# Pooled and local attention with a SoLU feed-forward layer on one core: the local probabilities of batches 3 to 7 transposed by DMA and VectorE instead of TensorE, with a new order of all engines

## The chip, the cores and the metric

The kernel runs on one core of one Trainium2 chip. The metric is the device time in microseconds (us) of one execution. The kernel before was timed three times: 622.41 us in the median, 622.0 lowest and 624.12 highest.

## The reference

Eight batches of eight heads, 576 positions, 64 values a head. Attention is computed twice and added: once between positions that were averaged in groups of four (144 of them, softmax over all, then each result repeated four times), and once locally, where a position sees only its neighbours at a distance below four.

```python
out_d = sm_attn(q_d, k_d, v_d)                      # 144 pooled positions
out_up = np.repeat(out_d, factor, axis=2)           # factor = 4
mask = np.abs(pos[:, None] - pos[None, :]) < factor
scores = np.where(mask, scale * q @ k.T, -1e9)
attn = softmax(scores)                              # local
attn_out = out_up + attn @ v
# x: 4608 tokens x 512
h = x @ w_in                                        # 512 -> 1024
solu = h * softmax(h)
ln = (solu - mean) / sqrt(var + 1e-6) * g_ln
out = ln @ w_out                                    # 1024 -> 512
```

The inputs are fp32, the feed-forward weights arrive as 64-bit words.

## The kernel before

**Local attention.** The 576 positions of a batch are covered by ten windows of 64, two windows to a unit, so five units a batch (class `Local`; a name such as `sc_3_1` is the local score tile of batch 3, unit 1). `by_tensor` (L690) makes a unit in these steps: 16 small matmuls for the scores into PSUM (`sc`, L698); on VectorE the mask is added (`pl`, L710) and the maximum taken (L715); GpSimd subtracts it (L717); ScalarE takes the exponential (L719); VectorE sums and inverts (L722, L726); GpSimd multiplies (L728). Then TensorE transposes the probabilities in four 128x128 pieces into PSUM (`plt`, L738), ScalarE copies them to SBUF (`plT`, L741), and 16 small matmuls multiply them with v (`xp`, L748). The result is written to x by ScalarE (`accumulate`, L587) or added by VectorE (L589). The rows of v for this form, `vw`, are loaded in four DMAs a unit with the two windows swapped for half of the heads (`load_vw`, L316).

A second form, `by_blocks` (L606), stands in the file but isn't used: `ON_TENSOR = 8` (L595) sends all eight batches through `by_tensor`.

**Pooled attention** (class `Pooled`): four units a batch, score tile `sd`, transposed tile `pdt`, result `po`. In batches 0 and 1 the pooled v comes from matmuls (`pv`, L490), later from GpSimd (`vs`, `vd`, L517 and L520). q and k are transposed on TensorE in batches 0 to 2 (`qp`, `kp`, L570), by VectorE's 32x32 transposes in batches 3 to 7 (L460, L464).

**Feed-forward.** 36 tiles of 128 tokens. Each is split into two parts of reduced width (`xh`, `xl`), multiplied in 24 matmuls of 512 columns (`h`, L848), normalised by all three vector engines, written to DRAM (`u`, L891) and read back in four DMAs as blocks (`v`, L924), which VectorE transposes (L945); after a split (`uh`, L951; `ul`, L953) 24 matmuls make the output (`o`, L967), which ScalarE scales (L974) and SyncE stores (L976). `v` has two buffers, `vw` five, `plT` two, the probabilities `pl` four.

**Order.** The work is a list of about two thousand steps, and the table `ORDER` gives the order in which they are written out; each engine executes its own in that order and waits for what is not ready. All DMAs are issued by SyncE, one queue in that same order: a DMA that waits holds up all DMAs behind it. The table `FILL` names PSUM tiles with a number n: ahead of the first matmul into such a tile, TensorE does n matmuls of the identity with itself (`idle_...`, L237) whose result nobody reads.

Of the kernel before, what the change touches and what calls it, by code (L numbers as in the profile page):

```python
# [139 lines left out]
def pooled_local_attention_then_solu_ffn(  # L140
# [451 lines left out]

    ON_TENSOR = 8  # L595

    class Local:

# [513 lines left out]
```

## Time and profile before

| | |
|---|---|
| time, median of 3 | 622.41 us (622.0 to 624.12) |
| time of the profiled execution | 623.45 us |
| its span, first to last instruction | 621.7 us |
| TensorE busy (matmul) | 599.2 us, 96% |
| VectorE, ScalarE, GpSimd busy | 391.9, 373.3, 374.5 us, 63%, 60%, 60% |
| moved by DMA | 91.97 MB, 148 GB/s in the mean |
| granted TensorE clock, mean | 0.989 |

The profile is of one execution. Busy time of TensorE is that of its matmul records; they overlap, so the time that a piece of work takes on TensorE is read from its start to the start of the next piece. An fp32 matmul can stand in the trace as two records: 16 local score matmuls give 32, and one `idle` matmul gives two. Matmuls of the reduced type (`h`, `o`) and transposes give one. SPq is SyncE issuing a DMA.

### The profile page before, as it was taken

To read this page: it belongs to the slowest core of one execution; us is meant where nothing else is said; L and a number is where in the kernel's file an instruction comes from. 1 tells how busy PE (TensorE), PEld (TensorE's weight loads), DVE (VectorE), ACT (ScalarE), POOL (GpSimd) and SP (SyncE) were. 2 spreads that over 40 slices of the span, in tenths; PEclk is the share of its full clock that TensorE was granted. 3 is DMA by queue.
4 is the path that set the end of the run, shared out by engine and by line. 5 is a ranking of instruction groups with operands and counts; after the bars stand their busy time and mean duration, and the time that the engine had idled before them with its cause. 6 is when DMAs were issued, how large, how long until landed. Compare 5 with 4: busy or idle time off the path is not lost.

```text
span 621.7 us, 15270 instructions
## 1 busy us (share of the span) xinstructions
PE 599.2 (96%) x5932; PEld 472.2 (76%) x5932; DVE 391.9 (63%) x687; ACT 373.3 (60%) x810; POOL 374.5 (60%) x566
## 2 busy tenths in 40 slices
PE   6969899999999999999999999999999999999997
PEld 5847768777777777777777877777777777788876
DVE  4877599997446784578537783778367444443540
ACT  4656668966556557556755585656655675454451
POOL 7553476769835895479636973689546964242210
PEclk9998799999999999999999999999999999999999
DMA  9969678987976279735883897433542232224220
GB/s 192 203 150 210 145 215 186 170 205 191 189 190 161 91 180 193 186 112 147 194 190 105 196 183 181 161 104 89 168 126 86 71 101 86 85 90 159 92 101 35
DMA packets 205608, 91.97 MB, mean 148 GB/s; under 512 B 169568, under 2 KB 194400, under 8 KB 205536
## 3 DMA queue, kind: packets, MB, share of 16 engines
q1 hardware_dynamic: 205536, 91.00, 60.5%
q8 instruction: 47, 0.77, 0.5%
q14 instruction: 25, 0.20, 0.1%
HBM read 63.18 MB, written 27.79 MB: 146 GB/s over the span
## 4 chain that ended last, share of the span: by engine, by line
PE 76%; POOL 7%; SPq 4%; DMA 4%; ACT 3%; DVE 3%; issue 2%; POOLq 0%; ACTq 0%
PE o L967 28%; PE h L848 28%; PE xp L748 3%; PE po L830 3%; PE sc L698 3%; PE plt L738 3%; SPq L316 3%; PE sd L774 2%; PE pdt L809 2%; POOL vs L517 1%; POOL pl L728 1%; POOL pl L717 1%; PE kp L570 1%; DMA v<-u 1%; PE pv L490 1%
## 5 line engine op out<-in xcount | busy, mean ns | idle before, releaser
L967 PE MATMUL o<-wo_h,uh 128*128 128x512 f32 x288 | 117.2, 407 | 0.3
L848 PE MATMUL h<-wi_h,xh 128*128 128x512 f32 x288 | 117.3, 407 | 0.0
L967 PE MATMUL o<-wo_l,uh 128*128 128x512 f32 x288 | 114.3, 397 | 0.0
L848 PE MATMUL h<-wi_l,xh 128*128 128x512 f32 x288 | 114.2, 396 | 0.0
L848 PE MATMUL h<-wi_h,xl 128*128 128x512 f32 x288 | 114.1, 396 | 0.0
L953 POOL TENSOR_TENSOR ul<-v,uh 128x512 fp32r<-128x512 f32 x58 | 74.5, 1291 | 27.2 <-ACT uh L951 25.3
L856 DVE TENSOR_REDUCE nmx<-h 128x1 f32<-128x1024 f32 x36 | 43.7, 1214 | 59.3 <-PE h L848 59.3
L967 PE MATMUL o<-wo_h,ul 128*128 128x512 f32 x288 | 79.0, 396 | 0.0
L967 PEld LDWEIGHTS o<-wo_h,uh 128*128 128x128 f32 x288 | 54.3, 189 | 13.7 <-issue 0.5
L848 PEld LDWEIGHTS h<-wi_h,xh 128*128 128x128 f32 x288 | 54.3, 188 | 13.5 <-issue 0.8
L967 PEld LDWEIGHTS o<-wo_h,ul 128*128 128x128 f32 x288 | 54.3, 189 | 13.3
L848 PEld LDWEIGHTS h<-wi_h,xl 128*128 128x128 f32 x288 | 54.3, 188 | 13.2
L848 PEld LDWEIGHTS h<-wi_l,xh 128*128 128x128 f32 x288 | 54.3, 189 | 11.6
L967 PEld LDWEIGHTS o<-wo_l,uh 128*128 128x128 f32 x288 | 54.3, 188 | 11.6
L1001 POOL TENSOR_TENSOR xl<-x,xh 128x512 fp32r<-128x512 f32 (+1 forms) x40 | 47.0, 1179 | 24.5 <-ACT xh L998 24.2
L728 POOL TENSOR_TENSOR pl<-pl,rsl 128x512 f32<-128x512 f32 x40 | 43.2, 1086 | 19.5 <-DVE rsl L726 13.4
L945 DVE STREAM_TRANSPOSE v<-v 128x512 f32<-128x512 f32 x70 | 46.3, 691 | 11.1 <-DMA v<-u 11.0
L860 ACT ACTIVATE e<-h,nmx 128x1024 f32<-128x1024 f32 x36 | 40.1, 1113 | 21.8 <-DVE nmx L856 21.4
L885 ACT ACTIVATE e<-e,nmu 128x1024 f32<-128x1024 f32 x35 | 40.2, 1148 | 20.5 <-POOL nmu L868 20.4
L951 ACT ACTIVATE uh<-v 128x512 fp32r<-128x512 f32 x70 | 43.5, 624 | 14.6 <-DVE v L945 11.6
L717 POOL TENSOR_TENSOR pl<-pl,mxl 128x512 f32<-128x512 f32 x40 | 42.9, 1079 | 15.1 <-DVE mxl L715 14.8
L998 ACT ACTIVATE xh<-x 128x512 fp32r<-128x512 f32 (+1 forms) x40 | 22.8, 584 | 46.8 <-PE h L848 39.5
(117 smaller groups left out, 1152.5 us busy)
## 6 DMA issues: line engine op xcount, KB each, us to landing
u<-e SPq DMA_DIRECT2D x35, 512.0 KB
v<-u SPq DMA_DIRECT2D x140, 128.0 KB
vw<-in_v_dram SPq DMA_DIRECT2D x160, 64.0 KB
out_dram<-osb SPq DMA_DIRECT2D x36, 256.0 KB
vs<-in_v_dram SPq DMA_DIRECT2D x24, 288.0 KB
qm<-in_q_dram SPq DMA_DIRECT2D x20, 288.0 KB
km<-in_k_dram SPq DMA_DIRECT2D x20, 288.0 KB
w<-in_moe_w_out_dram SPq DMA_DIRECT2D x8, 512.0 KB
```

Of the source, the lines that this page charges most:

```text
L717: nc.gpsimd.tensor_tensor(out=pl, in0=pl, in1=max_bc, op=ALU.subtract)
L728: nc.gpsimd.tensor_tensor(out=pl, in0=pl, in1=rs.unsqueeze(3).broadcast_to([P, NPR, 2, W]), op=ALU.mult)
L848: nc.tensor.matmul(hps[:, n, :], src[:, cc, :], wt[:, cc, n * 512:(n + 1) * 512], start=(cc == 0 and src is xh and wt is wi_h), stop=(cc = ...
L856: nc.vector.tensor_reduce(out=nmx, in_=hf, op=ALU.max, axis=AX.X, negate=True)
L860: nc.scalar.activation(e, hf, AF.Exp, bias=nmx, scale=1.0, accum_out=se)
L885: nc.scalar.activation(e, e, AF.Identity, bias=nmu, scale=1.0)
L945: nc.vector.transpose(vg, vg)
L951: nc.scalar.activation(uh, tp, AF.Copy)
L953: (nc.vector if v is None or i in LATE else nc.gpsimd).tensor_tensor(out=ul, in0=tp, in1=uh.bitcast(F32), op=ALU.subtract)
L967: nc.tensor.matmul(o, src[:, j, :], wt[:, 4 * g + j, :], start=(g == 0 and j == 0 and src is uh and wt is wo_h), stop=(g == 1 and j == 3 a ...
L998: nc.scalar.activation(h, src, AF.Copy)
L1001: nc.gpsimd.tensor_tensor(out=l, in0=src, in1=h.bitcast(F32), op=ALU.subtract)
```

## The change

Batches 3 to 7 use `by_blocks`; batches 0 to 2 stay as they were. In `by_blocks` the scores are written to PSUM in another arrangement, so that each 32 keys of all heads lie together (L610 to L631); the steps up to the product on GpSimd are the same in number and size, with one small VectorE instruction more (1e-9 added to the sums, L649 before). The transposition differs: eight DMAs of 32 partitions by 256 elements move the 32x32 blocks to their places in SBUF (L660 before, L661 after), and one VectorE transpose of 128x512 turns each block in itself (L666, L667). TensorE's four `plt` transposes and ScalarE's copy go. The `xp` matmuls then take 64 columns instead of 56 or 58. v's rows are loaded as they lie, in two DMAs a unit instead of four, the same bytes (L308, L309). All lines behind the tables are one higher in the program after.

```diff
 FILL = {
-    "kp_0_2": (3, "o"), "qp_0_3": (2, "o"), "kp_0_3": (2, "o"), "pv_0_1": (3, "o"),
-    "po_0_0": (8, "o"), "sd_0_2": (2, "o"), "po_0_3": (3, "o"), "plt_0_0": (12, "o"),
-    "xp_0_0": (5, "o"), "sc_0_1": (6, "o"), "sc_0_3": (13, "o"), "xp_0_3": (2, "o"),
-    "o_2": (6, "o"), "pv_1_0": (2, "o"), "sc_1_0": (3, "o"), "sc_1_2": (2, "o"),
-    "plt_1_2": (8, "o"), "xp_1_2": (4, "o"), "sc_1_3": (3, "o"), "po_1_3": (3, "h"),
-    "plt_2_2": (10, "o"), "o_34": (3, "h"), "o_35": (5, "h"),
+    "qp_0_1": (11, "o"), "kp_0_1": (5, "o"), "qp_0_2": (3, "o"), "kp_0_3": (3, "o"),
+    "pv_0_0": (2, "o"), "pv_0_1": (10, "o"), "pdt_0_0": (2, "o"), "sd_0_1": (3, "o"),
+    "pdt_0_1": (3, "o"), "sd_0_2": (3, "o"), "plt_0_0": (4, "o"), "xp_0_0": (6, "o"),
+    "xp_0_2": (7, "o"), "xp_0_4": (2, "o"), "h_1": (2, "o"), "h_3": (4, "o"),
+    "pv_1_0": (7, "o"), "sc_1_2": (5, "o"), "xp_1_3": (2, "o"), "pdt_1_0": (9, "o"),
+    "sd_1_2": (9, "o"), "sd_1_3": (3, "o"), "po_1_3": (4, "h"), "o_4": (8, "o"),
+    "o_8": (15, "o"), "qp_2_2": (3, "o"), "pdt_2_1": (3, "o"), "o_14": (13, "o"),
+    "pdt_4_1": (3, "o"), "o_34": (3, "h"), "o_35": (5, "h"),
 }
...
-0 33 7 14 1 2 3 21 4 5 8 6 135 40 9 143 10 41 42 15 151 11 12 16 13 17 28 43 18 19 44 22 20 50
+28 33 29 0 135 30 1 143 2 3 31 136 4 5 6 34 137 7 138 139 144 140 40 145 141 146 14 41 142 42
...
-    ON_TENSOR = 8
+    ON_TENSOR = 3
```

The new table changes all engines' order. The numbers at the end of a name below only count the program's tiles.

TensorE in batch 3, between feed-forward tile 8's first half and tile 6's second, before:

```order
L848 MATMUL h_8_3015<-wi_h_113,xh_8_2647 128x512
L848 MATMUL h_8_3015<-wi_l_114,xh_8_2647 128x512
L848 MATMUL h_8_3015<-wi_h_113,xl_8_2648 128x512
L748 MATMUL xp_3_0_3072<-plT_3_0_3028,vw_3_0_2209 64x58 x16
L698 MATMUL sc_3_4_3095<-kT_3_2171,qT_3_2170 64x64 x16
L738 MATMUL plt_3_1_3119<-ident_82,pl_0_103 128x128 x4
L967 MATMUL o_6_3128<-wo_h_115,uh_6_0_2947 128x512
```

The same place after:

```order
L849 MATMUL h_8_3049<-wi_h_113,xh_8_2652 128x512
L849 MATMUL h_8_3049<-wi_l_114,xh_8_2652 128x512
L849 MATMUL h_8_3049<-wi_h_113,xl_8_2653 128x512
L672 MATMUL xp_3_0_3104<-plT_3_0_2831,vw_3_0_2235 64x64 x16
L616 MATMUL sc_3_4_3127<-kT_3_2232,qT_3_2231 64x2x32 x16
L968 MATMUL o_6_3155<-wo_h_115,uh_6_0_3012 128x512
L968 MATMUL o_6_3155<-wo_l_116,uh_6_0_3012 128x512
```

The row of the four transposes is gone; `xp` has 64 columns and the scores go out in two stripes of 32.

SyncE's queue around the read-back of tile 8 (`v_8`), ahead of the q and k loads of batch 5, before:

```order
L891 DMA u_8_3187<-e_8_3141 128x1024
L316 DMA vw_4_1_3219<-in_v_dram 64x4x64 x4
L924 DMA v_8_3265<-u_8_3187 32x4x256 x4
L976 DMA out_0_dram<-osb_6_3209 128x512
L296 DMA qm_5_3295<-in_q_dram 32x72x32 x4
L296 DMA km_5_3296<-in_k_dram 32x72x32 x4
```

And after:

```order
L892 DMA u_8_3240<-e_8_3170 128x1024
L309 DMA vw_4_1_3254<-in_v_dram 64x8x64 x2
L977 DMA out_0_dram<-osb_6_3249 128x512
L661 DMA plT_3_3_3278<-pl_2_105 32x256 x8
L325 DMA vs_4_1_4_3370<-in_v_dram 72x4x256
L661 DMA plT_3_4_3377<-pl_3_106 32x256 x8
L892 DMA u_9_3422<-e_9_3374 128x1024
L309 DMA vw_4_2_3447<-in_v_dram 64x8x64 x2
L977 DMA out_0_dram<-osb_7_3445 128x512
L925 DMA v_8_3482<-u_8_3240 32x4x256 x4
L925 DMA v_9_3505<-u_9_3422 32x4x256 x4
L297 DMA qm_5_3514<-in_q_dram 32x72x32 x4
```

`v_8` went from two places behind `u_8` to nine: two groups of eight block DMAs, the write of tile 9 and the store of tile 7 stand in between. `o_8` has 15 fill matmuls ahead of it in the new table, and none before.

SyncE's first DMAs, before:

```order
L552 DMA qm_0_124<-in_q_dram 96x6x64 x2
L552 DMA km_0_125<-in_k_dram 96x6x64 x2
L552 DMA qm_0_124<-in_q_dram 96x6x64 x2
L552 DMA km_0_125<-in_k_dram 96x6x64 x2
L552 DMA qm_0_124<-in_q_dram 96x6x64 x2
```

And after:

```order
L317 DMA vw_0_0_124<-in_v_dram 64x4x64 x4
L317 DMA vw_0_1_161<-in_v_dram 64x4x64 x4
L553 DMA qm_0_166<-in_q_dram 96x6x64 x2
L553 DMA km_0_167<-in_k_dram 96x6x64 x2
L363 DMA stage_172<-in_moe_w_in_dram 64x1024 x2
```

Eight DMAs of v's rows moved ahead of the first q and k. Further down, the loads of batch 1's first three `vw` stand behind one piece of w_out (`w64_10`) and one `vs` more than before.

193 rows, old and new, of the table ORDER are left out of this document.

## The prediction

> **What bounds the kernel now.** I read the page first, then the busy time of the engines in four stages, then TensorE's and SyncE's timelines at single places. The page names TensorE:
>
> ```profile
> span 621.7 us, 15270 instructions
> PE 599.2 (96%) x5932; PEld 472.2 (76%) x5932; DVE 391.9 (63%) x687; ACT 373.3 (60%) x810; POOL 374.5 (60%) x566
> ```
>
> I cut the span where the first and the fifth feed-forward tile (h_0, h_4) begin on TensorE, 80.90 and 144.19 us:
>
> ```profile
> 80.90 0.50 PE L848 MATMUL h<-wi_h,xh 128*128 128x512 f32 x1
> ...
> 144.19 0.48 PE L848 MATMUL h<-wi_h,xh 128*128 128x512 f32 x1
> ```
>
> By the order of both programs TensorE does the same 972 matmuls, fill left out, ahead of h_4. So the change can be counted stage by stage. Busy time by stage, with the granted clock, the DMA share and GB/s at the end of a row:
>
> ```profile
> 0.00:80.90 80.90, 66.58 (x950) 54.09 (x950) 55.12 (x102) 45.90 (x121) 44.00 (x69) 0.92 0.94 182
> 80.90:144.20 63.30, 62.08 (x737) 48.84 (x735) 57.14 (x96) 49.96 (x92) 44.24 (x56) 1.00 0.83 192
> 144.20:510.00 365.80, 362.82 (x3685) 284.12 (x3683) 234.43 (x419) 226.18 (x510) 255.89 (x371) 1.00 0.60 150
> 510.00:621.70 111.70, 107.69 (x567) 85.19 (x566) 45.16 (x72) 51.24 (x90) 30.37 (x73) 1.00 0.27 90
> ```
>
> Up to 80.9 us TensorE idles 14.3 us and runs at 0.92 of its clock: this stage waits for loads (DMA share 0.94). From 144.2 us on it idles 3.0 of 365.8 us: there the time is what TensorE has to do, and all batches that the change touches lie there.
>
> **The change part by part.** *The transposes that go.* A slot between two feed-forward tiles looks like this:
>
> ```profile
> 214.55 0.69 PE L748 MATMUL xp<-plT,vw 64*64 64x58 f32 x32
> 215.06 0.65 PE L698 MATMUL sc<-kT,qT 64*64 64x64 f32 x32
> 215.65 0.66 PE L738 MATMUL plt<-ident,pl 128*128 128x128 f32 x4
> 216.06 0.47 PE L967 MATMUL o<-wo_h,uh 128*128 128x512 f32 x1
> ```
>
> From start to start plt takes 216.06 - 215.65 = 0.41 us, a unit. Five batches of five units: 25 x 0.41 = 10.25 us less on the engine that bounds this stage.
>
> *Wider xp.* 58 columns take 0.51 us here, the 64-column scores 0.59. By columns, 0.51 x 64/58 gives 0.05 more; the ends are 0 and 0.08. I take 0.04: 25 x 0.04 = 1.0 us (0 to 2.0). The scores keep their number and width.
>
> *Fill in this stage.* Before, 16 fill matmuls stand behind h_4, ahead of plt_2_2 and o_2:
>
> ```profile
> 151.08 2.50 PE L237 MATMUL idle_plt<-ident 128*128 128x128 f32 x20
> 154.55 0.66 PE L738 MATMUL plt<-ident,pl 128*128 128x128 f32 x4 [0.97 <-POOL pl L728]
> 155.04 1.50 PE L237 MATMUL idle_o<-ident 128*128 128x128 f32 x12
> 156.70 0.47 PE L967 MATMUL o<-wo_h,uh 128*128 128x512 f32 x1
> ```
>
> They go, and with them (154.55 - 151.08) + (156.70 - 155.04) = 5.1 us; it is 0 if the waits below them stay, which GpSimd's 0.97 us hints at. I take the 5.1, as the order has other work there. The new table puts 42 into this stage (o_4 8, pdt_2_1 3, o_8 15, pdt_4_1 3, o_14 13). Ten took 2.50 us, so 0.25 each: 42 x 0.25 = 10.5 us. Fill costs its time whether TensorE would have waited there or not; it is lost either way, and a longer wait adds to it. So this one term eats the whole of the 10.25.
>
> Is there a wait under it? For o_8 I think so. In the new order v_8 is issued behind the store of tile 7; from the end of o_7 the chain is ScalarE's output 0.68, four issues, the landing, two VectorE transposes 2 x 0.69, the first split 0.62. The rows, from the groups of instructions (busy, mean ns, idle before), SyncE's timeline and the chain that ended last:
>
> ```profile
> L967 PEld LDWEIGHTS o<-wo_h,uh 128*128 128x128 f32 x288 | 54.3, 189 | 13.7 <-issue 0.5 <-ACT osb L974 0.5
> L945 DVE STREAM_TRANSPOSE v<-v 128x512 f32<-128x512 f32 x70 | 46.3, 691 | 11.1 <-DMA v<-u 11.0
> L951 ACT ACTIVATE uh<-v 128x512 fp32r<-128x512 f32 x70 | 43.5, 624 | 14.6 <-DVE v L945 11.6
> ...
> 258.65 1.92 SPq L924 DMA_DIRECT2D v<-u  x4
> ...
> 260.15 6.03 DMA v<-u
> ...
> 209.02 5.61 PE h L848 x24
> ```
>
> With 1.92 for the issues and a landing between 2 (a choice, low) and 6.03 us: 0.7 + 1.9 + 2 to 6 + 1.4 + 0.6 = 6.6 to 10.6 us. TensorE has h_10 meanwhile, 5.6 us, and four small groups (xp, sd, xp, pdt) of about 0.5 us as in the slot above, 7.6 us; the fill's 15 x 0.25 bring it to 11.4. So the fill covers the wait and I add none.
>
> *The other engines.* VectorE gets 25 transposes of 0.69 us (row L945, the same tile size) and 25 small sums, 0.2 us by the row of the 128x8 reciprocal:
>
> ```profile
> L726 DVE RECIPROCAL rsl<-sml 128x8 f32<-128x8 f32 x40 | 8.1, 203 | 1.4
> L741 ACT ACTIVATE plT<-plt 128x512 f32<-128x512 f32 x40 | 23.7, 592 | 7.6 <-PE plt L738 7.4
> L728 POOL TENSOR_TENSOR pl<-pl,rsl 128x512 f32<-128x512 f32 x40 | 43.2, 1086 | 19.5 <-DVE rsl L726 13.4
> L1001 POOL TENSOR_TENSOR xl<-x,xh 128x512 fp32r<-128x512 f32 (+1 forms) x40 | 47.0, 1179 | 24.5 <-ACT xh L998 24.2
> ```
>
> That is 22 us on an engine that is busy 234 of 365.8 us; ScalarE loses 25 x 0.59 = 15 us. Both are under TensorE's work: zero. If VectorE waits for a late block transfer, the maximum of the next h tile stands behind it in its order, which is part of the first rival. GpSimd's two steps keep their size; with the other stride they cost between their 1.09 and the 1.18 us of a subtraction of two full operands, 25 x 2 x 0.09 = 5 us on an engine with 110 us to spare.
>
> *SyncE.* Each unit adds eight block DMAs of 32 KB. Nearest are the four pieces of v<-u, 128 KB each: 1.92 / 4 = 0.48 us an issue; and the four of vw, 64 KB each, 2.58 / 4 = 0.65. So it isn't the size that sets it, and I take 0.48: 3.8 us a unit (to 5.2). v's rows in half as many issues save between 0 (if it goes by rows) and 1.3 us:
>
> ```profile
> 416.76 2.58 SPq L316 DMA_DIRECT2D vw<-in_v_dram  x4
> ...
> SPq L891 <- ACT e L885: 133.7, 22, 12.1
> SPq L976 <- ACT osb L974: 37.3, 18, 7.8
> SPq L324 <- POOL vd L520: 25.0, 9, 5.6
> SPq L924 <- DMA u<-e: 19.8, 16, 2.7
> ```
>
> So 25 x (2.5 to 5.2) = 62 to 130 us more in the queue, against 215.8 us that it spends in these four waits. In the sum it fits: zero, with the first rival as the price if it doesn't. The Trainium skill speaks against this: "DMA: Bandwidth & Descriptors", Anatomy of one DMA, gives about 2.0 us of fixed cost to a DMA, and its Rules for kernel authors say that below 64 KB one mostly pays overhead; as an estimate from that page, eight paid one after another are 16 us a unit, 400 us in all, some 184 more than these waits hold, and the time would be near 800 us. The row of four pieces in 1.92 us shows that they are issued without paying that in turn, so the sum goes by the row.
>
> *The early stages.* Eight vw DMAs, 2 x 2.58 = 5.2 us, stand ahead of the first q load, so TensorE starts about 5 us later. 23 fill matmuls more stand ahead of h_0 and 3 more up to h_4 (26 x 0.25 = 6.5 us). Against this: two of the waits before h_0, and a halved clock twice:
>
> ```profile
> 46.58 4.55 PE L490 MATMUL pv<-vw,sums 64*72 64x256 f32 x20 [4.07 <-ACT vd L502]
> ...
> 68.51 0.85 PE L748 MATMUL xp<-plT,vw 64*64 64x58 f32 x42 [2.19 <-issue]
> ...
> 40.00:60.00 20.00, 15.64 (x143) 11.01 (x140) 11.78 (x22) 9.68 (x29) 5.89 (x5) 0.83 1.12 209
> 60.00:80.00 20.00, 17.17 (x382) 14.67 (x382) 12.37 (x25) 12.31 (x31) 10.02 (x9) 0.83 0.75 169
> ```
>
> What fixes h_0, I think, is the pv group of batch 1 just ahead of it on TensorE in both orders: it needs batch 1's first three vw. Ahead of these the new queue has a w_out piece and a vs more:
>
> ```profile
> vw<-in_v_dram SPq DMA_DIRECT2D x160, 64.0 KB
> vs<-in_v_dram SPq DMA_DIRECT2D x24, 288.0 KB
> w<-in_moe_w_out_dram SPq DMA_DIRECT2D x8, 512.0 KB
> ```
>
> 512 + 288 KB are 4.4 us at the stage's 182 GB/s. But vw runs at SyncE's pace, 64 KB in 0.65 us or some 100 GB/s, so part of it hides. Ends: -9 us (waits and clock gone, the late start absorbed) and +10 (late start and fill paid in full). I take a value near the middle, as the same loads end the stage: +0.6, and 3 x 0.25 = 0.75 up to h_4.
>
> *Sum:* -10.25 + 1.0 - 5.1 + 10.5 + 0.6 + 0.75 = -2.5 us. The profiled execution took 623.45 us, 1.75 beside its span, so 620.9 on its scale; it lies 1.04 above the median of the three. On the median: 622.41 - 2.5 = 619.9, said as 620.0 us.
>
> **The rivals.** *Slower: the one DMA queue.* By the new order 11 of the 25 groups of block DMAs stand directly ahead of a v<-u group. Each holds it up for 3.8 us, plus the time it waits itself for GpSimd's product: 42 us if no tile had slack. For slack speaks that the list of TensorE's waits has none for a split v (uh); against it, that VectorE waits for v already, for 11 of 35 tiles:
>
> ```profile
> DVE v L945 <- DMA v<-u: 11.0, 11, 2.7
> ```
>
> If a quarter of the 42 gets through, 10 us: 630 us. It decides where a read-back has less than 3.8 us in hand. Chance 0.25.
>
> *Faster: fill replaces idle time and keeps the clock.* If TensorE's 4.07 us wait goes (v is there early) and the two stretches at 0.83, 2 x 0.17 x 20 = 6.8 us of clock, go too, stage one is 4.07 + 6.8 - 5.2 = 5.7 us shorter instead of 0.6 longer: 613.6 us. For it: 10 fills instead of 3 at that very pv. Against it: the stage ends with loads. The Trainium skill, "TensorE: Matmul & The Clock Gate", HAM oscillation, says that an idle stretch above some 3.4 us halves the clock; the trace agrees at the 4.07 us wait, and by it this rival is what the denser fill would do. Chance 0.2.
>
> *No change at all,* because the transposes lay under other work, I hold for excluded: TensorE idles 3.0 us in 365.8. Nor can the change fail to do what it says; the order shows the rows gone.
>
> **How the numbers follow.** Forecast 0.5: a band of about 6 us around 620.0, of which 0.26 lies below 620.5, 0.15 within 0.3% of 622.41 (620.5 to 624.3, what a measurement of this kernel can just tell apart), 0.09 above. Slower rival 0.25, all above. Faster rival 0.2, all below. The rest of 0.05 goes 0.03 to the same and 0.02 to slower. Faster 0.46, same 0.18, slower 0.36. Low end 609: the faster rival's 613.6, less the 1.0 for xp and 3.6 of the late start. High end 632: the slower rival's 630 and xp's upper end with another microsecond of early fill. Outside remain less than 2 in 10.
>
> **What would show it.** Right: between h_4 and the end the span shrinks by 3 to 5 us; a slot without plt is 0.4 us shorter; the o_8 fill is followed by little idle time; h_0 starts at 79 to 85 us. Wrong: TensorE waits for uh or for plT in the list of waits, several us each, with SyncE's waits on the block DMAs in front (the slower rival); or h_0 starts by 76 us with a clock of 1.0 from 40 to 80 us (the faster one). I am wrong in the sign's ground if fill in the new profile covers nothing, that is, if the operands of o_8 and o_14 were ready long before the fill ended.

## The result and the profile after

The changed kernel takes 632.53 us in the median of four runs (630.18 to 634.61), the kernel before, run beside it, 622.2 us: a ratio of 1.0145, 95% interval 1.0107 to 1.0182. It is slower by about 10 us; the forecast was 620.0, within 609 to 632.

The profiled execution took 630.18 us, the shortest of the four, so its span shows 6.4 us of the 10. The page of the changed kernel (span, busy time, the chain that ended last by engine):

```profile
span 628.1 us, 15648 instructions
PE 599.5 (95%) x5936; PEld 471.1 (75%) x5936; DVE 423.6 (67%) x737; ACT 360.5 (57%) x785; POOL 376.8 (60%) x566
PE 62%; SPq 14%; DVE 8%; DMA 7%; ACT 3%; POOL 3%; issue 3%; DVEq 0%; POOLq 0%; ACTq 0%
```

TensorE is busy as long as before, 599.5 against 599.2 us, though 100 transposes are gone: fill took their place. SyncE issuing DMAs is 14% of the chain that ended last, with the block DMAs as SyncE's largest part, 5%.

The busy time by stage shows where the 6.4 us came from. The cuts are h_0, h_4, h_17 on TensorE. After (a row: stretch, length, busy time of TensorE, its weight loads, VectorE, ScalarE, GpSimd; clock, DMA share, GB/s):

```profile
0.00:83.09 83.09, 67.42 (x997) 55.62 (x997) 59.77 (x104) 46.76 (x121) 44.23 (x68) 0.96 0.91 179
83.09:149.50 66.41, 63.63 (x745) 49.74 (x741) 56.69 (x99) 51.72 (x95) 50.61 (x66) 1.00 0.75 183
149.50:353.44 203.94, 199.89 (x2003) 155.99 (x2002) 142.24 (x253) 111.66 (x254) 130.35 (x188) 1.00 0.70 168
353.44:628.10 274.66, 268.52 (x2206) 209.74 (x2200) 164.95 (x284) 150.33 (x316) 151.65 (x246) 1.00 0.49 136
```

The two later stages of the kernel before, with the new cut at its own h_17:

```profile
144.19:343.56 199.37, 196.92 (x1996) 154.16 (x1994) 130.20 (x232) 120.21 (x270) 135.82 (x198) 1.00 0.69 165
343.56:621.70 278.14, 273.61 (x2259) 215.16 (x2257) 149.40 (x260) 157.21 (x329) 150.45 (x246) 1.00 0.41 116
```

Stage by stage: 83.09 - 80.90 = +2.2 us, 66.41 - 63.29 = +3.1, 203.94 - 199.37 = +4.6, 274.66 - 278.14 = -3.5. So the change gains in the last stage, where 14 of the 25 units stand, and loses in all three ahead of it, in the third although 11 units' transposes went there too. Within the third stage the loss stands at three tiles, those with fill ahead of their `o`: from h_6 to h_7 (o_4) it takes 3.7 us longer than before, from h_10 to h_11 (o_8) 4.7 and from h_16 to h_17 (o_14) 2.4; the tiles between them are shorter by 6.1 us in sum. The second profile of the changed kernel (run e12 below) has the same shape: h_4 7.0 us behind the kernel before, h_17 12.7, the end 9.3.

A slot without the transposes, on TensorE's timeline after:

```profile
220.16 0.69 PE L672 MATMUL xp<-plT,vw 64*64 64x64 f32 x32
220.68 0.65 PE L616 MATMUL sc<-kT,qT 64*64 64x64 f32 x32
221.26 0.51 PE L968 MATMUL o<-wo_h,uh 128*128 128x512 f32 x1
```

The 0.41 us of plt are gone, and the wider xp takes 220.68 - 220.16 = 0.52 us, against 0.51 before. The waits that changed, from the list of waits after:

```profile
PE qp L571 <- POOL sums L265: 10.0, 1, 10.0
DVE v L946 <- DMA v<-u: 20.4, 12, 3.3
ACT uh L952 <- DVE v L946: 22.4, 15, 4.6
```

TensorE starts at 10.0 instead of 4.40 us. VectorE waits 20.4 us for read-backs, 11.0 before, ScalarE 22.4 for VectorE's transposed v, 11.6 before. SyncE's queue at the point that the prediction worked out, the read-back of tile 8 (the last row holds those of tiles 8 and 9, four DMAs each):

```profile
236.54 4.94 SPq L661 DMA_DIRECT2D plT<-pl  x8
242.23 0.33 SPq L892 DMA_DIRECT2D u<-e  x1
242.60 2.50 SPq L309 DMA_DIRECT2D vw<-in_v_dram  x2
245.19 0.57 SPq L977 DMA_DIRECT2D out_dram<-osb  x1
245.80 3.81 SPq L925 DMA_DIRECT2D v<-u  x8
```

Eight block DMAs take 4.94 us, 0.62 each, not 0.48; the trace's 25 groups take 4.94 to 7.69 us, 137 in sum. The two issues of vw take 2.50 us here, nearly the 2.58 of four before, but this place is an exception: over the 25 units two issues take 1.27 to 2.64 us, 41.6 in sum, where the four of before took 2.57 to 3.78, 72.9 in sum. And what TensorE does meanwhile, with the fill at o_8:

```profile
248.98 0.53 PE L810 MATMUL pdt<-ident,pd 64*72 64x64 f32 x12
249.44 3.62 PE L238 MATMUL idle_o<-ident 128*128 128x128 f32 x30
253.21 0.48 PE L968 MATMUL o<-wo_h,uh 128*128 128x512 f32 x1
```

The fill is followed by 0.15 us of idle time: it is about as long as the wait below it. ScalarE's split for o_8 (`uh_8`) ends 0.37 us before o_8 begins; in the kernel before, without fill, it ended 8.2 us before. Which work makes it late is the question of the experiments.

A step that can make it late shows in ScalarE's order at tile 14 (instructions in sequence, the lists of the two programs). Before:

```
L951 ACTIVATE uh_14_0_4710<-v_14_4611 128x512
L951 ACTIVATE uh_14_1_4721<-v_14_4611 128x512
L860 ACTIVATE e_16_4756,se_16_4757<-h_16_4662,nmx_16_4718 128x1024
```

After:

```
L861 ACTIVATE e_16_4827,se_16_4828<-h_16_4723,nmx_16_4784 128x1024
L817 ACTIVATE pdT_4_3_4825<-pdt_4_3_4812 72x6x48
L952 ACTIVATE uh_14_0_4833<-v_14_4756 128x512
L901 ACTIVATE e_15_4588,m2_15_4837<-e_15_4588 128x1024
L952 ACTIVATE uh_14_1_4842<-v_14_4756 128x512
```

The split of tile 14, which TensorE needs for o_14, stood ahead of the exponential of tile 16 and stands behind it now; the same has happened to uh_8 and the exponential of tile 10, and to uh_4 and that of tile 6. Behind h_4 these are the only three tiles of the new order whose split stands behind the exponential of two tiles later, and o_4, o_8 and o_14 are the only `o` behind h_4 to which the new table adds fill. That exponential can't begin until TensorE has finished h_16, and o_14 comes right behind h_16. ScalarE's timeline there, changed kernel (in brackets the idle time before, and what ended it):

```profile
342.77 1.12 ACT L861 ACTIVATE e<-h,nmx 128x1024 f32<-128x1024 f32 x1 [3.84 <-DVE nmx L857]
343.79 0.19 ACT L861 ACTIVATION_READ_ACCUMULATOR e<-h,nmx 128x1 f32 x1
343.88 0.39 ACT L817 ACTIVATE pdT<-pdt 72x288 f32<-72x288 f32 x1
344.17 0.62 ACT L952 ACTIVATE uh<-v 128x512 fp32r<-128x512 f32 x1
344.69 1.05 ACT L901 ACTIVATE e<-e 128x1024 f32<-128x1024 f32 x1
345.73 0.62 ACT L952 ACTIVATE uh<-v 128x512 fp32r<-128x512 f32 x1
```

So behind h_16 TensorE needs VectorE's maximum (1.2 us) and then 1.12, 0.19, 0.39 and 0.62 us of ScalarE before its operand is there, while the small groups of the slot last 1.7 us. A wait of about the difference is thus written into the order; the 13 fill matmuls at o_14 lie on it. They last longer than it: the split ends at 344.79 us, the fill 1.4 us later.

### The profile page after: what moved, and what is told of

It is laid out like the page before. It is cut to its first block, busy times and chain, and to the rows that moved or that the text cites. A ratio compares the mean times of both kernels' runs of the same rounds, so it can differ in the third digit from the quotient of the medians.

```text
span 628.1 us, 15648 instructions
## 1 busy us (share of the span) xinstructions
PE 599.5 (95%) x5936; PEld 471.1 (75%) x5936; DVE 423.6 (67%) x737; ACT 360.5 (57%) x785; POOL 376.8 (60%) x566
## 4 chain that ended last, share of the span: by engine, by line
PE 62%; SPq 14%; DVE 8%; DMA 7%; ACT 3%; POOL 3%; issue 3%; DVEq 0%; POOLq 0%; ACTq 0%
PE o L968 24%; PE h L849 23%; SPq L661 5%; SPq L317 4%; SPq L553 2%; DMA v<-u 2%; PE po L831 2%; PE xp L672 2%; PE pdt L810 2%; PE sd L775 1%; SPq L925 1%; PE sc L616 1%; DMA u<-e 1%; DMA vs<-in_v_dram 1%; DVE nmx L857 1%
## 5 line engine op out<-in xcount | busy, mean ns | idle before, releaser
L952 ACT ACTIVATE uh<-v 128x512 fp32r<-128x512 f32 x70 | 43.3, 624 | 30.0 <-DVE v L946 22.4
L946 DVE STREAM_TRANSPOSE v<-v 128x512 f32<-128x512 f32 x70 | 46.6, 693 | 20.4 <-DMA v<-u 20.4
L901 ACT ACTIVATE e<-e 128x1024 f32<-128x1024 f32 x35 | 36.8, 1052 | 17.6 <-DMA u<-e 17.6
L864 DVE SCALAR_TENSOR_TENSOR e<-h,e 128x1024 f32<-128x1024 f32 x36 | 43.4, 1206 | 4.9 <-ACT e L861 4.6
L799 POOL TENSOR_TENSOR pd<-pd,rsd 128x432 f32<-128x432 f32 x32 | 30.0, 938 | 26.4 <-DVE rsd L797 25.4
```

What stands on the lines that cost most here:

```text
L864: nc.vector.scalar_tensor_tensor(out=e, in0=hf, scalar=1.0, in1=e, op0=ALU.mult, op1=ALU.mult, accum_out=su)
L901: nc.scalar.activation(e0, e, AF.Square, accum_out=m2)
L946: nc.vector.transpose(vg, vg)
L952: nc.scalar.activation(uh, tp, AF.Copy)
```

## The experiments

Ratios are to the kernel before, run on the same chip in the same set, with the 95% interval; its medians there were 622.1 to 623.87 us. "The changed kernel" is the one above. Nine profiles with the order and fill of the changed kernel up to h_4 (the start of e2 aside) reach h_4 at 149.1 to 152.5 us, so a difference of 2 or 3 us between two totals can come from there, and the places where TensorE waits say more.

**e1: the middle fill taken out** (the entries that leave FILL).

```diff
-"o_4": (8, "o"), "o_8": (15, "o"), "pdt_2_1": (3, "o"), "o_14": (13, "o"), "pdt_4_1": (3, "o"),
```

> The changed kernel without the 42 fill matmuls that stand behind h_4 (o_4, pdt_2_1, o_8, pdt_4_1, o_14). Theory: most of this fill covers a real wait for the read-back of a feed-forward tile (in the changed kernel's trace the first split of tile 8 ends at 252.8 us and its fill at 253.1; tiles 4 and 14 are ready 1.4 us before their fill ends), so only about 3 us come back: 629 us, and TensorE shows the waits in place of the fill. Rival: the fill is what costs, 42 x 0.25 = 10.5 us: 622 us.

634.7 us, 1.0191 (1.014 to 1.0241). Neither number came: it isn't faster at all, so that fill costs nothing; it stands on waits. TensorE at o_14 in this run shows what the fill does for its 3.3 us:

```profile
345.71 0.53 PE L810 MATMUL pdt<-ident,pd 64*72 64x64 f32 x12
348.01 0.50 PE L968 MATMUL o<-wo_h,uh 128*128 128x512 f32 x1 [1.77 <-ACT uh L952]
...
349.04 0.42 PE L968 MATMUL o<-wo_h,uh 128*128 128x512 f32 x1
349.27 0.61 PE L968 MATMUL o<-wo_l,uh 128*128 128x512 f32 x1
349.68 0.63 PE L968 MATMUL o<-wo_h,uh 128*128 128x512 f32 x1
...
352.92 0.40 PE L968 MATMUL o<-wo_h,uh 128*128 128x512 f32 x1
...
355.35 0.71 PE L831 MATMUL po<-pdT,vd 72*64 72x144 f32 x8
```

The bare wait is 1.77 us, but 1.3 us after its end the products come 0.43 us apart instead of 0.235, for 3.4 us: the 24 take 355.35 - 348.01 = 7.34 us, with the fill 5.78. The wait and the lower clock behind it, 1.77 + 1.56, are 3.33 us, the length of the fill.

**e12: the changed kernel once more**, as a yardstick for other sets.

> The changed kernel itself, on the chip of this set, as the yardstick for the three others: 631 to 634 us by every theory.

634.78 us, 1.0179 (1.0137 to 1.0221); e1 and this can't be told apart.

**e2: the first q and k loads ahead of the vw loads** in SyncE's order.

```diff
-28 33 29 0 135 30 1 143
+0 28 33 29 135 30 1 143
```

> The changed kernel with batch 0's first q and k loads put back ahead of the eight v loads in SyncE's queue, nothing else moved. Theory: the first matmul comes about 5 us earlier (4.5 instead of 10.0 us) and, since the early stage then ends with the loads of batch 1 that are the same bytes, at most half of that reaches the end: 630 us. Rival, that the late start is paid in full: 627 us. Rival, that it is absorbed: 632.5 us.

634.71 us, 1.0195 (1.0142 to 1.0249). TensorE starts at 4.12 us, 5.9 earlier, and h_0 still begins at 84.86 us. The late start is absorbed before h_0.

**e3 and e8: the new order with TensorE's transposes.** In e3 plt stands where the block DMAs were issued, its copy right behind, and the middle fill stays; in e8 plt and copy stand 22 and 16 steps ahead of xp, about as before, without the middle fill.

```diff
-    ON_TENSOR = 3
+    ON_TENSOR = 8
```

> The changed kernel's order and fill, but all batches transposed on TensorE as before (the copy of the transposed tile right behind the transposes, v's rows in four DMAs). Theory that the order and the fill cost and the new transposition by itself pays: the 10.25 us of transposes come back on top, less what the fill had covered: 636 to 642 us. Rival, that the block DMAs in SyncE's queue cost more than the transposes they replace: faster than the changed kernel, 622 to 630 us, since the queue is rid of 25 x 5 us.

> The new order without its middle fill, with all local probabilities transposed on TensorE as before, its transposition and copy put as far ahead of the probability product as they stand in the kernel before (22 and 16 steps), not where the DMAs are issued as in the earlier run, which gave 650 us. Theory 1, the new order by itself is slower than the old: 640 to 650 us, near the earlier run. Theory 2, the earlier run was slow only because TensorE waited in its own order for probabilities that weren't ready: 627 to 634 us.

e3 649.76 us, 1.0437 (1.0383 to 1.0492); e8 643.19, 1.0319 (1.0274 to 1.0364). Part of e3's loss was the early place of plt or the middle fill on top of it; e8, without both, is 6.6 us faster. What is left is the new order with the old transposition, 3% over the old order. And e8 beside e1, the same order with and without block transposition: 1.0319 against 1.0191, about 8 us. On TensorE behind h_4 e8 has 11.9 us more of plt, start to start, and 3.0 us less of fill and idle time. So the transposition pays about what -10.25 + 1.0 says, less some waits, and the order that came with it costs more than twice as much. That price holds with plt where I put it, which need not be its best place.

**e4b: the old order with block transposition**, the DMAs right behind GpSimd's product and VectorE's transpose half-way to xp.

```diff
-    ON_TENSOR = 8
+    ON_TENSOR = 3
```

> The order and fill of the kernel before, with the transposition by block DMAs from batch 3 on; the DMAs are issued right behind GpSimd's product, the VectorE transpose half way between its old copy's place and the product with v. Theory that the order costs and the transposition pays: 622 - 9 = 613 us, up to 618 if VectorE waits for some blocks. Rival, that the queue is the cost: 25 groups of 5 us of issues delay the read-backs, TensorE waits for them: above 626 us.

717.97 us, 1.151 (1.1431 to 1.159). Its waits:

```profile
DVE v L945 <- DMA v<-u: 59.7, 16, 9.8
PE xp L671 <- issue: 36.3, 9, 8.0
SPq L660 <- POOL pl L653: 33.0, 12, 6.2
```

Here the mechanism of the prediction's slower rival is in full view: SyncE stands 33 us with block DMAs for the product of GpSimd, VectorE 59.7 us for read-backs behind them (11.0 in the kernel before), and TensorE waits at xp. From the first of its DMAs to VectorE's transpose a block unit takes 6.6 to 12.2 us in the changed kernel, where plt took 0.66 and its copy 0.59. With the new steps at these places the old order loses 15%, so the change needs its steps elsewhere; whether smaller moves than the new table would do was not tried here.

**e5: the early part as before.** Steps up to h_4 in the old order with the old fill, the rest new.

```diff
-"qp_0_1": (11, "o"), "kp_0_1": (5, "o"), ...
+"kp_0_2": (3, "o"), "qp_0_3": (2, "o"), ...
```

> The changed kernel, in which every step up to the first product of tile 4 (h_4) stands in the order of before, with the fill of before; all later steps keep the new order and the new fill, and the block transposition stays. Theory 1, the early order costs: the traces put h_4 at 149.5 us in the changed kernel and at 144.2 us before, 5.3 us apart, and these stay to the end: 627 us (626 to 629). Theory 2, what comes after h_4 sets the end, and an early start is taken back by later waits, as in the run with the q load first: 631 to 635 us.

634.57 us, 1.017 (1.0119 to 1.0221). h_4 begins at 142.24 us, 7.3 us ahead of the changed kernel's profile, but h_5 at 168.27, 1.5 behind it. So the early order and fill do set h_4, and the lead is gone one tile behind the joint of the two orders, where TensorE stands 4.9 us in o_2 for GpSimd's second halves (`ul`). Whether the new order there or the joint makes that wait this run can't say; in the changed kernel o_2 waits 2.4 us for the same, and the joint in e10 costs much too.

**e6: no block DMAs** (on e1's base, shortened here). VectorE transposes straight from pl, so the exchange of the off-diagonal blocks is left out.

```diff
-                        nc.sync.dma_start(plT[...], pl[...])
...
-            nc.vector.transpose(flat, flat)
+            nc.vector.transpose(flat, pl)
```

> The changed kernel without its middle fill (as in the run without it, 634.7 us) and without the 200 block DMAs: VectorE transposes the 32x32 blocks straight from pl, at the same place in the order, so the two off-diagonal blocks of each 64x64 probability tile do not change places. This leaves out part of the computation. Theory 1, the queue costs: SyncE loses 25 times about 5 us of issuing, the scratch trips of u and v come back earlier, and the waits that the middle fill covered go: 622 to 627 us. Theory 2, the new order itself leaves the gaps, whatever SyncE does: 632 to 635 us.

631.61 us, 1.0129 (1.0085 to 1.0172), against e1's 1.0191; the intervals overlap, and from h_4 to h_35 the profiles are 2.8 us apart. All 200 DMAs away are worth some 3 us. So the queue alone isn't the cause, and the rival's price of 10 us for it, in this order, is three times too high. TensorE at o_8 in e1, then at o_8 and o_14 in this run:

```profile
253.82 0.79 PE L968 MATMUL o<-wo_h,uh 128*128 128x512 f32 x1 [3.56 <-ACT uh L952]
255.90 0.72 PE L961 MATMUL o<-wo_h,uh 128*128 128x512 f32 x1 [3.40 <-ACT uh L945]
348.64 0.50 PE L961 MATMUL o<-wo_h,uh 128*128 128x512 f32 x1 [1.70 <-ACT uh L945]
```

Without any block DMA TensorE waits for the same split as long as with them: 3.40 and 1.70 us, against 3.56 and 1.77 in e1. ScalarE's order there is unchanged, the exponential of tile 16 (346.57 us in this run), then the split of tile 14 (347.96).

**e7 and e11: the middle tiles nearer to their old places** (on e1's base). e7 moves the read-backs of tiles 4, 8 and 14; e11 also their transposes and the halves of u, all to the places in the list that they have in the kernel before. In SyncE's queue only v_8 thereby passes other DMAs (the queue, not the code):

```diff
+v_8<-u_8 x4
 vs_4_1_4
 plT_3_4<-pl x8
 u_9<-e_9
 vw_4_2 x2
 out_0_dram<-osb_7
-v_8<-u_8 x4
```

> The changed kernel without its middle fill, and with the read-back of v for tiles 4, 8 and 14 moved ahead in SyncE's order, to the distance from the tile's last first-layer product that it has in the kernel before (tile 8: 47 steps earlier, ahead of block DMAs that stood before it). Theory 1, the late place of these three read-backs is what the middle fill covered (10.5 us, 7 of them at o_8 and o_14 and 2 at o_4): 625 to 629 us. Theory 2, the block DMAs moved behind the read-backs come late in their place, and the probability product waits instead: 632 to 637 us.

> The changed kernel without its middle fill; the read-back of v, its transposes, and the high and low halves of u (steps 14 to 20 of tiles 4, 8 and 14) stand at the places in the order that they have in the kernel before, not only the read-back as in the earlier run. Theory 1, the late halves of u on ScalarE and GpSimd are what o_4, o_8 and o_14 wait for (the trace shows ScalarE's uh of tile 8 behind the square sum of tile 9 and the exp of tile 10): the waits go, 625 to 629 us beside 634.7 with the fill merely taken out. Theory 2, other chains end within 2 us of these, and the waits move on: 631 to 636 us.

634.32 us, 1.0179 (1.0125 to 1.0233), and 634.52, 1.0173 (1.0129 to 1.0217): no change. In e7 o_8 waits 2.7 us for ScalarE's split, still behind the exponential of tile 10. In e11 the split comes ahead of it, but its v is read back behind the block DMAs of unit 3_3, and now the probability product of the slot before waits 5.3 us. At o_14 the read-back of both still stands behind the DMAs of unit 5_0: e7, with the late split, waits 2.19 us, and e11, with the split ahead of the exponential, 2.36, as the split now waits 5.9 us for VectorE's transposed v.

**e16 and e18: read-backs ahead of block DMAs.** e16 is e1 with v_14 ahead of unit 5_0's DMAs; e18 is e11 with that and v_8 ahead of unit 3_3's (again the queue).

```diff
+v_14<-u_14 x4
 plT_5_0<-pl x8
-v_14<-u_14 x4
```

> The changed kernel without its middle fill, with the read-back of v for tile 14 placed directly ahead of the 8 block DMAs of unit 5_0, not behind them; nothing else moves. In the changed kernel's chain at o_14 SyncE issues these DMAs in 4.5 us from the probabilities' product on, then the read-back, and o_14 follows. Theory 1, the one queue makes that wait: the time from h_16 to h_17, 18.0 us without the fill and 15.5 before, falls to 15 us, and the total by about 3 us, to 631 or 632 us. Theory 2, ScalarE's order or another chain ends just behind: no change there, 634 to 635 us.

> The run with the middle tiles as before (no middle fill, 634.5 us), with the read-back of v for tile 8 directly ahead of the block DMAs of unit 3_3 and that of tile 14 ahead of those of unit 5_0. In that run's chain SyncE issues 8 block DMAs from 232.2 to 237.2 us, then the read-back of v for tile 8, whose halves keep ScalarE from the work that the next probability product waits for (5.3 us). Theory 1, the queue: 7 to 10 us less, 624 to 628 us. Theory 2, the waits move on once more: 631 us or more.

e16: 632.76 us, 1.0125 (1.0072 to 1.0178), with h_16 to h_17 at 19.9 us, longer than e1's 18.0: o_14 waits 3.65 us. The queue alone didn't make that wait; theory 1 of this run falls, though the total fits it (h_4 came 1.6 us earlier than in e1, in the same order). e18: 633.67, 1.0145 (1.0089 to 1.0201). With the split ahead of the exponential *and* the read-back ahead of the DMAs the waits do go: h_16 to h_17 takes 14.6 us (e1 18.0, before 15.5), h_10 to h_11 16.8 (e1 20.4, before 14.4). But h_9 to h_10 is 1.9 us longer than in e1 and h_14 to h_15 3.9 us (19.4 against 15.5): there TensorE waits 2.7 us at sd, behind VectorE's transpose of a plT that had just landed. From h_4 to h_35 e18 is only 0.6 us shorter than e1. So at o_14 the split early alone (e11), the read-back early alone (e16) and neither (e1) leave waits of 2.36, 3.65 and 1.77 us, and both together leave none: the wait has two causes that end within a microsecond or two. The work pushed back waits elsewhere.

**e9, e13, e17: blocks from batch 5 on.** The old order and fill for the first 1180 of 2072 steps, then the new order; e13 and e17 move one read-back each ahead of a group of block DMAs (v_15 past unit 5_1, v_14 past 5_0).

```diff
-    ON_TENSOR = 3
+    ON_TENSOR = 5
```

> The order and fill of before for its first 1180 of 2072 steps, the new order for the rest, and block transposition only for batches 5, 6 and 7 (15 of the 25 units), which lie wholly behind the cut. Theory 1, the changed kernel loses its time in the order of the middle tiles (4.65 us at o_8, 3 at o_14, 5 up to tile 7) and gains where the transpositions go without a new wait: from tile 21 to tile 28 it takes 2.9 us off the lead of before (9.45 to 6.55): 617 to 620 us beside 622. Theory 2, the block DMAs cost a wait wherever they stand, or the joint of the two orders does: 624 us or more.

> The run with blocks from batch 5 on, with one step moved: the read-back of v for tile 15 stands ahead of the 8 block DMAs of unit 5_1 instead of behind them. In that run's trace SyncE waits 6.4 us with these DMAs for the probabilities, issues them in 5.1 us, and only then reads v back; TensorE stands 7.6 us at o_15 and its next 24 products take 8.5 instead of 5.8 us. Theory 1, the one queue is the cause there: the 7.6 + 2.7 us go, 617 to 620 us beside 622 to 624 of before. Theory 2, another chain ends just behind: 624 to 628 us, as without the move (628.6).

> The run with blocks from batch 5 on (628.6 us), with the read-back of v for tile 14 placed directly ahead of the block DMAs of unit 5_0. Theory 1, the one queue makes the wait at o_14 there (7.6 us, and 2.7 us of lower clock behind it): 618 to 620 us beside 622 to 624 of before. Theory 2, another chain ends just behind: 625 to 629 us.

628.58 us, 1.0077 (1.0045 to 1.0109); 629.54, 1.0105 (1.0079 to 1.0132); 628.27, 1.0068 (1.0038 to 1.0099). In e9 TensorE waits 7.6 us at o_14, with SyncE in front:

```profile
332.68 5.03 SPq L660 DMA_DIRECT2D plT<-pl  x8
337.76 2.00 SPq L924 DMA_DIRECT2D v<-u  x4
```

I took that v for tile 15's; it is tile 14's, so e13 moved the wrong one. e17 moved the right one, and o_14 still waits 6.75 us. VectorE in e17:

```profile
337.20 0.20 DVE L651 RECIPROCAL rsl<-sml 128x8 f32<-128x8 f32 x1
339.81 0.71 DVE L666 STREAM_TRANSPOSE plT<-plT 128x512 f32<-128x512 f32 x1 [2.40 <-DMA plT<-pl]
340.44 0.12 DVE L894 RECIPROCAL r<-se 128x1 f32<-128x1 f32 x1
340.49 1.20 DVE L856 TENSOR_REDUCE nmx<-h 128x1 f32<-128x1024 f32 x1
```

And ScalarE in e17:

```profile
341.78 1.11 ACT L860 ACTIVATE e<-h,nmx 128x1024 f32<-128x1024 f32 x1 [5.53 <-DVE nmx L856]
342.79 0.19 ACT L860 ACTIVATION_READ_ACCUMULATOR e<-h,nmx 128x1 f32 x1
342.88 0.39 ACT L816 ACTIVATE pdT<-pdt 72x288 f32<-72x288 f32 x1
343.18 0.62 ACT L951 ACTIVATE uh<-v 128x512 fp32r<-128x512 f32 x1
```

The block DMAs reach o_14 on a second way: VectorE waits 2.40 us with the transpose of plT, the maximum of tile 16 stands behind it, ScalarE's exponential waits for that maximum, and the split of tile 14 stands behind the exponential. In e9 the second way ended 0.32 us ahead of the first: that long the split stood there for VectorE's transposed v, with the exponential and pdT already done. So taking the first way off brought 0.8 us of wait, 7.56 to 6.75.

**e10 and e14: blocks from batch 6 on**, cut at step 1400; e14 also puts the read-back, transposes and halves of tile 18, which stood right behind one another at the joint, at their old places.

```diff
-    ON_TENSOR = 3
+    ON_TENSOR = 6
```

> As the run with blocks from batch 5 on, cut at step 1400, and with block transposition for batches 6 and 7 alone (10 units, 10 x 0.41 = 4.1 us of TensorE less, 2 us given back in wider products and waits). Theory 1: 619 to 621 us beside 622, a little less gain than from batch 5 on. Theory 2: 624 us or more.

> The run with blocks from batch 6 on, with the read-back of v of tile 18, its transposes and the halves of u at the places of the kernel before (at the joint of the two orders they stood directly behind one another, and the trace shows 2.6 us of wait at pdt and 1.5 us of lower clock). Theory 1: the block transposition of 10 units pays once the joint's wait is gone, 617 to 620 us, 0.5% or more under the kernel before. Theory 2: its gain is taken back by later waits, 621 to 624 us, no different from before.

e10: 622.62 us, 0.9988 (0.9963 to 1.0012), with 4.7 us lost at the joint between h_19 and h_21. e14: 620.42 us, 0.9964 (0.9941 to 0.9987): a little faster than the kernel before, by about as much as can be told. Its stages, cut at its own h_4 and h_17:

```profile
142.72:343.03 200.31, 196.91 (x1995) 154.24 (x1994) 130.20 (x232) 120.27 (x270) 135.79 (x198) 1.00 0.69 163
343.03:618.50 275.47, 270.03 (x2219) 211.62 (x2217) 162.23 (x280) 151.44 (x319) 150.51 (x246) 1.00 0.46 127
```

The last stage is 278.14 - 275.47 = 2.7 us shorter than before, for ten units: 10 x 0.41 = 4.1, less 1.2 us more of fill and idle time and 0.25 for the wider xp.

**e15: blocks from batch 4 on**, cut at step 935, with tile 9's transposes and halves as before.

```diff
-    ON_TENSOR = 3
+    ON_TENSOR = 4
```

> The order and fill of before up to step 935, then the new order, blocks from batch 4 on (20 of 25 units); the transposes and halves of tile 9 stand as in the kernel before. Theory 1, the loss of the changed kernel lies before tile 11 (the trace puts h_11 9.2 us behind, and only 0.7 us is lost from there to tile 17): 617 to 621 us. Theory 2, the order of the tiles 11 to 17 costs as well (the middle fill at o_14 covers a real wait): 624 to 630 us.

626.75 us, 1.0052 (1.0028 to 1.0075). Up to h_14 it runs 2.6 us ahead of the kernel before, at h_17 it is 7.7 behind: 10.3 us lost over three tiles, 6.5 of them from h_14 to h_15, where e18 loses too (TensorE waits 3.0 us at sd), and 2.4 from h_16 to h_17, where e9 does. Theory 1 falls: what the new order does from tile 11 to 17, with blocks from batch 4 on, costs as well.

## Why the prediction was wrong, point by point

*What bounds it.* TensorE's work after h_4, right; but it was taken for the only thing there. TensorE waited for almost nothing in that stage because the old order kept its operands early (uh_8 8.2 us ahead of its product). That was a property of the order, which the change replaced.

*Transposes, xp, the fill's price.* The transposes that went came to 10.4 us, added up start to start after h_4 (predicted 10.25), the wider xp to 0.7 (1.0), 30 records of fill to 3.62 us (15 x 0.25 = 3.75). e1 against e8 shows that this part pays, with plt where e8 has it.

*Fill and waits after h_4.* "So the fill covers the wait and I add none" was right at o_8, to 0.15 us, but the chain below it was another: not the read-back alone, which the prediction followed, but ScalarE's order. But -5.1 for the old fill "as the order has other work there" was too good: fill and idle time together rose, start to start, from 6.45 to 14.8 us between h_4 and h_17, and by another 1.8 behind h_17. I had set +5.4 for the whole; it was +10.1. In the third stage its 8.3 us stand against 4.6 us of transposes that went there.

*SyncE.* 0.48 us an issue was too low: 0.62 in the group quoted, 137 us in the 25 groups against 25 x 3.8 = 95, while vw saved 72.9 - 41.6 = 31 us, the upper end of what was set. The 105 us that are left lie within the 62 to 130 said. So the size isn't what failed. The estimate of 16 us a unit from the Trainium skill ("DMA: Bandwidth & Descriptors", Anatomy of one DMA) didn't come, 4.94 to 7.69 us did; that section is on DMAs that GpSimd issues, and these are SyncE's. "In the sum it fits: zero": waits are at places, and a sum over the program doesn't say whether the eight DMAs fit in front of one read-back. e6 prices the DMAs at some 3 us in this order; in the old one, where e4b put them, the whole change cost 15%.

*VectorE, ScalarE, GpSimd: zero.* This is the step that failed behind h_4. Their busy time changed about as said (VectorE +31.7 us for 22, ScalarE -12.8 for -15), but each does its work in a fixed order, and that order was changed. In place of zero the runs show waits of 3.56 and 1.77 us at o_8 and o_14 under the fill (e1), as long without the DMAs (e6). The rows of ScalarE's order, there to be read before, put uh_14 behind the exponential of tile 16, uh_8 behind that of tile 10 and uh_4 behind that of tile 6; I followed only the read-back of v through SyncE. The sentence that VectorE's wait for a block transfer would hold up the next maximum was in the text as a part of the rival; e17 shows it, 2.40 us there and 5.53 on ScalarE behind it.

*The early stages.* This term failed too. +0.6 and +0.75 were +2.2 and +3.1 (e12's profile: h_4 7.0 behind), and the one profile of the kernel before flatters them: the nine profiles with its early order have h_4 at 142.2 to 144.2 us, the eleven with the new one at 149.1 to 152.5, some 8 us apart in the median. The late start is absorbed (e2). From TensorE's first product to h_0 the fill added 4.2 us and idle time fell by 4.1; between h_0 and h_4 each rose by 1.5. The value near the middle of -9 to +10 was a choice, without a row for it.

*The rivals.* The slower one had the right sign and nearly the size (630) and half the mechanism: block DMAs ahead of read-backs do hold them up, but taken away they free 3 us only. So its size was luck in good part: 10 us for the queue stood in for the order's waits and the early stages. The faster one came true in its clock, 0.96 instead of 0.92 up to h_0, and not in its time. The Trainium skill ("TensorE: Matmul & The Clock Gate", HAM oscillation) sets the danger at idle gaps above some 3.4 us. Here 1.77 us of idle time (e1, o_14) were enough for some 3.4 us at about half the pace, and 2.54 us (e8, o_8) were not, so the measurement goes further than the page.

*What stays open.* No single edit within the new order gave back more than 3 us of its loss, and the pair in e18 only moved it. That the new order loses with either transposition is shown (e1, e8), and that it gains where only batches 6 and 7 follow it (e14); what each of its places would give back if mended isn't, nor which steps of the early part cost its 8 us. Nor is it shown whether another order could give the gain of batches 3 to 5, or whether the new early part is needed by what follows.

## What to carry to other kernels

When a change takes work off the engine that bounds a kernel but gives it a path with a longer latency, price the order that has to make room for that path: for each operand of the bounding engine, list what stands ahead of its maker on every in-order engine, not only in the DMA queue. Ask of fill ahead of a product whether it marks a wait that somebody found there; where it does, as in e1, the time stays lost when the fill is taken out. And try such a change on the late part alone: here ten of 25 units, with the old order up to them, gave 0.4%, all 25 in a new order cost 1.4%.

## What the runs showed of the hardware

- A wait of TensorE can cost more than its length. Waits of 1.77 (e1, o_14) and 2.67 us (e7, o_8) were followed by about 3.4 us at a granted clock of 0.5, in which 128x512 products came 0.43 us apart, not 0.235. The 24 products behind e7's wait at o_8, and behind its wait of 2.19 us at o_14, with the granted clock:

```profile
253.09:260.44 7.35, 7.35 (x25) 5.58 (x25) 1.99 (x4) 2.77 (x4) 4.16 (x5) 0.77 1.26 197
347.51:353.32 5.81, 5.80 (x24) 4.44 (x24) 3.49 (x7) 2.39 (x5) 4.97 (x9) 1.00 0.46 116
```

The first took 7.35 us at a clock of 0.77, where the changed kernel's took 5.79. The second took 5.81 at 1.00, and so did those behind 1.70 us in e6 (o_14) and 2.54 in e8 (o_8). So fill over a wait of 1.8 to 3.6 us saves up to some 1.56 us; which waits are followed by the lower clock isn't shown here.
- SyncE's issue time doesn't follow the bytes: in the changed kernel's trace one issue takes, in the median, 0.59 us for a 32 KB block DMA inside SBUF, 0.43 for a 128 KB piece of v and 0.67 for 128 KB of vw, where 64 KB of vw took 0.61 before. So the same rows of vw in two DMAs instead of four took 41.6 us instead of 72.9.
